# Retention and two feed-forward layers on one core: the first units in a new order, and two steps moved to ScalarE

## The chip, the cores and the metric

One NeuronCore of a Trainium2 chip runs the whole kernel. Its engines have in-order queues of their own and meet only at semaphores: TensorE (PE in the rows; PEld is its weight load), VectorE (DVE), ScalarE (ACT), GpSimd (POOL) and SyncE (SP), which here mostly issues DMAs. The metric is device time in microseconds (us). Times inside an execution come from one profiled execution and are counted from the start of its span.

## The reference

Three stages follow each other; all weights and activations are float32 with 4 batches, 8 heads, 768 positions, head size 64, so 3072 tokens of 512 features.

```
state = gamma[h] * state + k_t^T v_t ;  y_t = scale * q_t state      (retention, per head)
x = y laid out [3072, 512]
h = x @ w_in            [512 -> 2048]
g = h if h > 0 else exp(h) - 1
x = g @ w_out           [2048 -> 512]
h = x @ w_in2           [512 -> 1024]
s = h * softmax(h) ;  ln = (s - mean(s)) / sqrt(var(s) + 1e-6) * g_ln
out = ln @ w_out2       [1024 -> 512]
```

## The kernel before, in words

**Precision.** A large matmul is three matmuls on rounded halves: high times high, low times high, high times low (`mm3`, lines 68 to 72). So each operand is split: the high half is a cast on ScalarE (`xh`, `gh`, `w1ih`, `zh`), the low half a subtraction on VectorE (`xl`, `gl`, `w1il`, `zl`). The weights come as 64-bit words and pass through five steps for each tile of 128x512: `load_w` (a 512 KB DMA into one of five buffers `raw`), `top_w` (a cast on ScalarE into `top`, then a memset on GpSimd), `bits_w` and `merge_w` (VectorE shifts and ors), `high_w` (ScalarE), `low_w` (VectorE). `order1` is the list of the first layer's 32 tiles: `w1i` 0, 1, 2, then `w1o` 0, `w1i` 3, `w1o` 1 and so on. In the texts w0 to w7 are the tiles by place in that list, so w3 is the first tile of the output weights.

**Retention** works on 48 units, each 64 positions of one batch, loaded as one 576 KB DMA (`load_unit`, u0, u1, ...). Units 0 to 3 are the first chunks of the four batches, 4 to 7 the second chunks, and so on. For a unit TensorE makes scores (S, line 199), then the products of keys and values (K, 206) and the outputs (V, line 249, and from unit 4 on also 246, which reads the state that the unit four places earlier left). VectorE masks the scores (M, 210), makes the state (C, 221 or 223) and scales the output into `xf` (D, 254). ScalarE copies two halves of the state (226), GpSimd scales the keys (R, 190) and decays the state (G, 233). Every fp32 matmul of the program shows in the trace as two passes, so a group of 8 stands there as x16. The first eight units share three sets of PSUM banks in turn (`ab` and two named `acc`).

**First layer.** A block is 512 tokens, that is eight units; the block's matmuls need all eight units, split into `xh` and `xl` (`split_x0` for block 0). A step s makes the input matmul of one group of 128 hidden features (`ff1_in`, 12 matmuls into `hp`), ScalarE and VectorE make the nonlinearity (`elu_a`, `elu_b`, `elu_c`), and two steps later `ff1_out` adds 12 matmuls into `acc`. In the first block's steps the weights are prepared (`prep_w`), and every second step holds one unit of the next block.

**Second layer** goes by 24 tiles of 128 tokens. `norm_a` is exp, sum and product, then the subtraction of the mean on GpSimd (line 394). `turn` transposes in 32x32 blocks on VectorE (414) and writes to DRAM (`t_dr`), `turned` reads it back with four DMAs (`zt`); `split_zh` and `split_zl` make the halves, and `ff2_out` is 24 matmuls into `op`. `split_y` makes the halves of a later tile's input, which `load_y` reads.

**What sets the order.** The program is recorded in the order in which the Python code runs, and each engine keeps that order. The first units are written by a loop over u (lines 491 to 508) with three tables, LOADS, MID and END, which say after which unit a load, a weight step or a split of x stands:

```
LOADS = {0: (2, 3, "0"), 1: (4,), 2: (5,), 3: (6,), 4: (7, "1"), 5: (8,), 6: ("2", "3", 9), 7: ("4", 10)}
```

(numbers are units, strings weight tiles). Between, the loop writes for each u, in this order: R and G of unit u+1, C of u, S and M of u+1, V of u, K of u+1, D of u. All loads go out on SyncE's queue.

Of the kernel before, what the change touches and what calls it, by code (L numbers as in the profile page):

```python
# [40 lines left out]
HALF_N = 232  # L41


@with_exitstack
def tile_retention_ffn(ctx, tc, qkv, w_in1, w_out1, w_in2, w_out2, g_ln, dmask, odec, kgdec, ident_in, out):
# [16 lines left out]
    g_sb = small.tile([P, NF2], F32, name="g_sb")  # L62
    half_n = small.tile([P, HALF_N], F32, name="half_n")[:, :1]

# [9 lines left out]
    with tc.manual_schedule():  # L74
# [20 lines left out]

        def load_w(x):
            t = stage_p.tile([P, 512, 2], U32, tag="raw", name="raw")
            nc.sync.dma_start(out=t.rearrange("p a b -> p (a b)"), in_=srcs[x[0]][x[1]].bitcast(U32))
            raw_t[x] = t
# [11 lines left out]
        quarter = lambda x, i, dt: raw_t[x].rearrange("p a b -> p (a b)").bitcast(dt).rearrange("p (a b) -> p a b", b=4)[:, :, i]  # L111

        def top_w(x):
            top = tops[-1][0]
            tops[-1].reverse()
            nc.scalar.copy(top.bitcast(F16).rearrange("p (a b) -> p a b", b=2)[:, :, 1], quarter(x, 3, BF16))
            nc.gpsimd.memset(quarter(x, 3, U16), 0)  # L117
            top_t[x] = top

        def bits_w(x):  # L120
            raw = raw_t.pop(x)
            low, t = raw[:, :, 0], raw[:, :, 1]
            nc.vector.scalar_tensor_tensor(low, low, 29, top_t.pop(x), ALU.logical_shift_right, ALU.bitwise_or)
            abs_t[x] = low, t
# [56 lines left out]

        def load_unit(u):
            pool, n = (first_p, 4) if u < 4 or u == UPB - 1 else (at_p, 3)
            t = pool.tile([P, 18 * D], F32, tag="in", name="in", bufs=n)
            nc.sync.dma_start(out=t, in_=qkv[u])
            in_t[u] = t
# [25 lines left out]

        def att_state(u, v):

            c = chunk(u)
            if c == NCH - 1:
                return
            st = at_p.tile([P, 2, 2 * D], F32, tag="state", name="state", bufs=B + 1)
            kv = v[:, :, 4 * C:4 * C + 2 * D]
            if c == 0:  # L220
                nc.vector.tensor_copy(st, kv)
            else:
                nc.vector.tensor_tensor(st, sg_t.pop(u), kv, ALU.add)
            s2 = at_p.tile([P, 2 * D], F32, tag="s2", name="s2", bufs=B + 1)
            for j in range(2):
                nc.scalar.copy(s2[half(1 - j)], st[half(j), 1 - j])
            s_t[u + B] = (st, s2)

# [6 lines left out]
        def att_values(u, banks):  # L235
            c = chunk(u)
            t, pt = in_t.pop(u), p_t.pop(u)
            col = lambda o: slice(2 * C + o * C, 2 * C + (o + 1) * C)
            by_kind = heads(lambda x, y, z: (y if x == 0 else 1 - y, y, z))
            if c > 0:  # L240
                st, s2 = s_t.pop(u)
# [137 lines left out]
        def norm_a(i):  # L379
# [12 lines left out]
            nc.vector.tensor_scalar(st[:, 5:6], st[:, 4:5], -1.0 / FF2, None, ALU.mult)  # L392
            if i < N2 - 1:
                nc.gpsimd.tensor_scalar(z, z, st[:, 5:6], 1.0, ALU.add, ALU.mult)  # L394
# [55 lines left out]
        def ff2_out(i, kks=range(NF2)):  # L450
# [13 lines left out]

        w = lambda f, i: lambda: step_w(f, order1, i)
        xh = lambda *us: lambda: split_x0(us, True)
        xl = lambda *us: lambda: split_x0(us, False)

        LOADS = {0: (2, 3, "0"), 1: (4,), 2: (5,), 3: (6,), 4: (7, "1"), 5: (8,), 6: ("2", "3", 9), 7: ("4", 10)}
        MID = {4: (w(bits_w, 0),), 5: (w(merge_w, 0),), 6: (xl(0, 1, 2, 3),)}  # L470
        END = {
            3: (w(top_w, 0), xh(0, 1, 2, 3)),
            5: (w(high_w, 0), xh(4, 5)),
            6: (xh(6),),
            7: (xh(7), w(low_w, 0), w(top_w, 1), xl(4, 5), xl(6), xl(7), w(bits_w, 1), w(top_w, 2), w(merge_w, 1)),
        }
        nc.gpsimd.memset(half_n, -0.5)
        new_top()
        nc.sync.dma_start(out=kg_sb, in_=kgdec)
        load_unit(0)  # L480
        nc.sync.dma_start(out=dm_sb, in_=dmask)
        load_unit(1)
        nc.sync.dma_start(out=od_sb, in_=odec)
        new_acc(0)
        sets = [([x[:, 0], x[:, 1]], x) for x in (ab, *acc_t[0])]
        both = sets[0]
        scale_k(0)
        att_scores(0, sets[0][0])
        att_mask(0, sets[0][1])
        att_kv(0, sets[0][0])  # L490
        for u in range(UPB):
            banks, v = sets[u % 3]
            nxt, w = sets[(u + 1) % 3] if u + 1 < UPB else both
            for x in LOADS.get(u, ()):
                load_unit(x) if isinstance(x, int) else step_w(load_w, order1, int(x))
            scale_k(u + 1)
            if u + 1 >= B:
                att_decay(u + 1)
            att_state(u, v)
            att_scores(u + 1, nxt)  # L500
            att_mask(u + 1, w)
            att_values(u, banks)
            att_kv(u + 1, nxt)
            for f in MID.get(u, ()):
                f()
            att_done(u, v)
            for f in END.get(u, ()):
                f()
# [3 lines left out]
        att_state(UPB, both[1])  # L512
        scale_k(UPB + 1)
        att_decay(UPB + 1)
        step_w(high_w, order1, 1)
        step_w(bits_w, order1, 2)
        step_w(low_w, order1, 1)
        slot = 1
# [3 lines left out]
        for s in range(NS + LAG):  # L522
# [12 lines left out]
            if u < NU:  # L535
# [13 lines left out]
                if u + 2 < NU:  # L549
                    scale_k(u + 2)  # L550
            if tb == 0:
                prep_w(order1, slot)
                slot += 1
# [11 lines left out]
            if tb == 0:  # L565
                prep_w(order1, slot)
                slot += 1
                elu_c(s, nc.vector)
            if s == HL:
# [33 lines left out]
        for i in range(1, N2):  # L603
# [92 lines left out]
```

## Time and profile before

| what | value |
|---|---|
| median of 3 runs | 875.2 us (874.94 to 876.35) |
| the profiled execution's own time | 874.49 us |
| its span | 872.7 us |
| TensorE busy | 857.3 us, 98% of the span, 6432 matmul passes |
| VectorE, ScalarE, GpSimd busy | 438.7, 330.6, 322.8 us |
| DMA moved | 97.81 MB |

A share of 98% is a mean over stages. TensorE's missing 15 us lie almost all at the beginning, where it waits for loads and for the other engines, a little at one place of the second layer, and at the end. Idle time of another engine costs nothing while TensorE has work.

### The profile page before, as it was taken

What the parts mean: (1) busy time and instruction counts of PE and PEld (TensorE: products, weight loads), DVE (VectorE), ACT (ScalarE), POOL (GpSimd) and SP (SyncE); (2) the same over time, 40 slices, a digit from 0 to 9 for tenths busy, and PEclk for the clock granted to TensorE, in tenths of its full rate; (3) what the DMA queues carried; (4) which work ended last, traced back from release to release, by engine and by line L of the source; (5) the groups of instructions that cost most, each with busy time, mean ns of one, the idle gap of its engine ahead of it and who ended that gap; (6) DMA issues with size and microseconds to landing.
All of it is one profiled execution on the core that took longest, in us unless ns stands there. A gap on an engine that the chain in (4) does not pass through costs nothing.

```text
span 872.7 us, 15630 instructions
## 1 busy us (share of the span) xinstructions
PE 857.3 (98%) x6432; PEld 702.8 (81%) x6432; DVE 438.7 (50%) x736; ACT 330.6 (38%) x575; POOL 322.8 (37%) x321
## 2 busy tenths in 40 slices
PE   6899999999999999999999999999999999999998
PEld 5788888888888888888888878888788888888887
DVE  4899983222522233222422268796555555555552
ACT  3677762222322233222321245443343333333333
POOL 4555533322323232332322245553443333333330
PEclk9999999999999999999999999999999999999999
DMA  8677623111311113110311116310644444444432
GB/s 331 229 232 236 206 98 104 56 46 37 103 56 55 36 48 104 56 55 29 102 56 31 55 67 205 97 48 1 200 150 145 145 146 145 145 145 145 145 122 71
DMA packets 59735, 97.81 MB, mean 112 GB/s; under 512 B 4880, under 2 KB 41360, under 8 KB 59664
## 3 DMA queue, kind: packets, MB, share of 16 engines
q1 hardware_dynamic: 59664, 96.82, 34.0%
q8 instruction: 50, 0.82, 0.4%
q14 instruction: 21, 0.17, 0.1%
HBM read 72.16 MB, written 24.64 MB: 111 GB/s over the span
## 4 chain that ended last, share of the span: by engine, by line
PE 91%; DMA 3%; DVE 3%; ACT 1%; issue 1%; SPq 0%; POOL 0%; ACTq 0%; DVEq 0%
PE hp L71 14%; PE hp L72 14%; PE hp L70 14%; PE acc L70 11%; PE acc L72 10%; PE acc L71 10%; PE op L72 4%; PE op L70 4%; PE op L71 4%; PE ab L199 2%; DMA in<-in_qkv 2%; PE ab L206 1%; PE ab L246 1%; PE ab L249 1%; DMA zt<-t_dr 1%; DMA t_dr<-t 1%
## 5 line engine op out<-in xcount | busy, mean ns | idle before, releaser
L323 POOL TENSOR_TENSOR gl<-e,gh 128x512 fp32r<-128x512 f32 x80 | 106.9, 1336 | 310.9 <-issue 158.1
L70 PE MATMUL acc<-gh,w1oh 128*128 128x512 f32 x384 | 153.9, 401 | 0.4 <-ACT w1oh L138 0.4
L72 PE MATMUL acc<-gh,w1ol 128*128 128x512 f32 x384 | 150.0, 391 | 0.2 <-DVE w1ol L146 0.2
L71 PE MATMUL acc<-gl,w1oh 128*128 128x512 f32 x384 | 149.8, 390 | 0.0
L71 PE MATMUL hp<-xl,w1ih 128*128 128x512 f32 x380 | 147.9, 389 | 0.4 <-DVE xl L267 0.4
L70 PE MATMUL hp<-xh,w1ih 128*128 128x512 f32 x380 | 147.9, 389 | 0.0
L72 PE MATMUL hp<-xh,w1il 128*128 128x512 f32 x380 | 147.8, 389 | 0.0
L304 ACT ACTIVATE e<-hp 128x512 f32<-128x512 f32 x80 | 47.8, 597 | 186.0 <-PE hp L72 186.0
L313 DVE TENSOR_SCALAR e<-e 128x512 f32<-128x512 f32 x80 | 38.5, 481 | 136.3 <-ACT e L304 136.1
L315 ACT CAST gh<-e 128x512 fp32r<-128x512 f32 x96 | 59.6, 621 | 95.1 <-DVE e L314 82.7
L70 PEld LDWEIGHTS acc<-gh,w1oh 128*128 128x128 f32 x384 | 72.0, 188 | 17.1 <-ACT w1oh L138 0.8
L72 PEld LDWEIGHTS acc<-gh,w1ol 128*128 128x128 f32 x384 | 72.1, 188 | 15.9 <-DVE w1ol L146 0.6
L210 DVE TENSOR_TENSOR pt<-ab,dm_sb 128x256 f32<-128x256 f32 x43 | 18.1, 421 | 131.1 <-PE ab L249 124.6
L71 PEld LDWEIGHTS hp<-xl,w1ih 128*128 128x128 f32 x380 | 71.3, 188 | 15.7 <-DVE xl L267 0.9
L71 PEld LDWEIGHTS acc<-gl,w1oh 128*128 128x128 f32 x384 | 72.1, 188 | 14.0
L72 PEld LDWEIGHTS hp<-xh,w1il 128*128 128x128 f32 x380 | 71.3, 188 | 14.8
L70 PEld LDWEIGHTS hp<-xh,w1ih 128*128 128x128 f32 x380 | 71.3, 188 | 14.8
L117 POOL MEMSET raw<- 128x512 uint16 x48 | 61.0, 1279 | 48.7 <-DVE w1il L146 18.2
L394 POOL TENSOR_SCALAR z<-z,st 128x1024 f32<-128x1024 f32 x22 | 27.8, 1263 | 138.2 <-DVE st L392 138.2
L72 PE MATMUL op<-w2oh,zl 128*128 128x512 f32 (+1 forms) x192 | 74.2, 386 | 1.4 <-DVE zl L435 1.4
L70 PE MATMUL hp<-w2ih,yh 128*128 128x512 f32 x192 | 74.7, 389 | 0.0
L71 PE MATMUL hp<-w2il,yh 128*128 128x512 f32 x192 | 74.7, 389 | 0.0
(118 smaller groups left out, 1411.7 us busy)
## 6 DMA issues: line engine op xcount, KB each, us to landing
in<-in_qkv SPq DMA_DIRECT2D x48, 576.0 KB, 4.2
raw<-in_w_in SPq DMA_DIRECT2D x24, 512.0 KB, 3.8
raw<-in_w_out SPq DMA_DIRECT2D x24, 512.0 KB, 4.1
t_dr<-t SPq DMA_DIRECT2D x22, 512.0 KB, 2.8
zt<-t_dr SPq DMA_DIRECT2D x88, 128.0 KB, 2.5
y_dr<-yt SPq DMA_DIRECT2D x24, 256.0 KB, 2.7
yin<-y_dr SPq DMA_DIRECT2D x24, 256.0 KB, 3.4
out<-ot SPq DMA_DIRECT2D x23, 256.0 KB, 2.8
```

Source lines behind the costliest of these rows:

```text
L70: nc.tensor.matmul(o, lh, rh, start=first, stop=False)
L71: nc.tensor.matmul(o, lh, rl, start=False, stop=False)
L72: nc.tensor.matmul(o, ll, rh, start=False, stop=last)
L117: nc.gpsimd.memset(quarter(x, 3, U16), 0)
L199: nc.tensor.matmul(banks[j][half(a), m * C:(m + 1) * C], blk(t, j, K, n), blk(t, j, Q, n), start=True, stop=True)
L206: nc.tensor.matmul(banks[a][half(j), 4 * C + m * D:4 * C + (m + 1) * D], blk(t, a, KR, n), blk(t, a, V, n), start=True, stop=True)
L210: nc.vector.tensor_tensor(pt, v[:, :, :2 * C], dm_sb, ALU.mult)
L304: nc.scalar.activation(e, h_t[s], AF.Exp)
L313: nc.vector.tensor_scalar(e, e, 1.0, -1.0, ALU.min, ALU.add)
L315: nc.scalar.copy(gh, e)
L323: engine.tensor_tensor(gl, e, gh.bitcast(F32), ALU.subtract)
L394: nc.gpsimd.tensor_scalar(z, z, st[:, 5:6], 1.0, ALU.add, ALU.mult)
```

## The change

The loop and its tables are replaced by one string of operations, START, which a table STEP maps to the functions; the letters are those used above, with L a unit's load, w a weight load, t, b, m, h, o the steps top, bits, merge, high and low, H and X the high and low split of x. `l` and `v` are a unit's and a weight's load issued from ScalarE's queue. A second string, LATER, stands in step 0 of the first layer. Parts that are new beside the order: the states of units 0 to 3 are copied out of PSUM by ScalarE and not by VectorE; the copies of state halves of units 4 to 8 are split off (`att_copy`) and put later; the loads of w4 and of unit 10 are issued by ScalarE; for every fourth tile of `order1` (places 1, 5, 9, ...) ScalarE makes the last bits with an activation in place, and the VectorE step `bits_w` falls away; and in the second layer tile 1's mean is subtracted by ScalarE, after `split_zl(0)`, with its transpose ahead of `split_y(3)`.

```
+START = """
+    n a z L0 k d L1 q L2 L3
+    R0 S0 M0
+    R1 S1 M1 V0 K0 C0 D0 L4 L5 w0
+    R2 S2 M2 V1 K1 C1 D1 L6 L7 H0 w1
+    R3 G4 S3 M3 V2 K2 C2 D2 H1
+    R4 S4 G5 M4 V3 K3 C3 D3 H2 t0
+    V4 D4 R5
+    S5 M5 K4 L8 C4 V5 R6 b0 S6 M6 m0 h0 K5 D5 G6 R7 H3 H4
+    S7 V6 M7 D6 V7 R8 t1 w2 H5 H6 D7 H7 C5 K6 C6 S8 K8 K7 X0,1 X2,3
+    o0 b1 m1 h1 X4,5 X6,7 t2 w3 L9 G8 G7 o1 b2 t3 M8 b3 C8 R9 c4 v4
+"""
+LATER = "m2 h2 C7 l10 G9"
...
         def top_w(x):
+            if x in order1[1::4]:
+                nc.scalar.activation(quarter(x, 0, U16), quarter(x, 1, U16), AF.Identity, bias=floor_n, scale=2.0 ** -13)
+                nc.scalar.copy(quarter(x, 1, F16), quarter(x, 3, BF16))
+                nc.gpsimd.memset(quarter(x, 3, U16), 0)
+                return
...
-            nc.vector.scalar_tensor_tensor(low, low, 29, top_t.pop(x), ALU.logical_shift_right, ALU.bitwise_or)
+            if x in top_t:
+                nc.vector.scalar_tensor_tensor(low, low, 29, top_t.pop(x), ALU.logical_shift_right, ALU.bitwise_or)
...
             if c == 0:
-                nc.vector.tensor_copy(st, kv)
+                nc.scalar.copy(st, kv)
...
+        def late_w(i):
+            done.add((load_w, order1[i]))
+            load_w(order1[i], nc.scalar)
...
+        for x in START.split():
+            STEP[x[0]](*(int(n) for n in x[1:].split(",") if n))
...
+            if s == 0:
+
+                for x in LATER.split():
+                    STEP[x[0]](*(int(n) for n in x[1:].split(",") if n))
+            if 0 < s < B + 1:
+                att_copy(B + s)
...
+                if s == 0:
+                    step_w(merge_w, order1, slot)
+                    step_w(high_w, order1, slot)
...
-            if i < N2 - 1:
+            if i == 1:
+                pass
+            elif i < N2 - 1:
                 nc.gpsimd.tensor_scalar(z, z, st[:, 5:6], 1.0, ALU.add, ALU.mult)
...
                 split_zl(0)
+                z, _, st = zc_t[1]
+                nc.scalar.activation(z, z, AF.Identity, bias=st[:, 5:6])
+                turn(1)
+                turned(1)
             if i + 2 < N2:
                 split_y(i + 2)
-            if i < N2 - 1:
+            if 1 < i < N2 - 1:
                 turn(i)
                 turned(i)
```

**TensorE just ahead of the first layer.** Before, the last groups of the first stretch (line 206 makes K, 199 S, 246 and 249 V) are, for units 5 to 8:

```order
L206 MATMUL ab<-in 64x64 x8
L199 MATMUL acc<-in 64x64 x8
L246 MATMUL ab<-in,state 64x64 x4
L246 MATMUL ab<-in,s_225 64x64 x4
L249 MATMUL ab<-pt,in 64x64 x8
L206 MATMUL acc<-in 64x64 x8
L199 MATMUL ab<-in 64x64 x8
L246 MATMUL acc<-in,state 64x64 x4
L246 MATMUL acc<-in,s_262 64x64 x4
L249 MATMUL acc<-pt,in 64x64 x8
L206 MATMUL ab<-in 64x64 x8
```

Now (222 is S, 229 K, 274 and 277 V):

```order
L222 MATMUL acc<-in 64x64 x8
L274 MATMUL ab<-in,state 64x64 x4
L274 MATMUL ab<-in,s_257 64x64 x4
L277 MATMUL ab<-pt,in 64x64 x8
L274 MATMUL acc<-in,state 64x64 x4
L274 MATMUL acc<-in,s_293 64x64 x4
L277 MATMUL acc<-pt,in 64x64 x8
L229 MATMUL ab<-in 64x64 x8
L222 MATMUL ab<-in 64x64 x8
L229 MATMUL ab<-in 64x64 x8
L229 MATMUL acc<-in 64x64 x8
```

The same groups stand there in all, but V of units 6 and 7 follow each other, and three K groups (units 6, 8 and 7) come last, ahead of the first `hp` matmul.

**ScalarE in the first steps.** In step 1 of the first layer, before (301 and 302 are the exponential of step 1's `hp`, 226 the state copies, 138 `high_w`, 116 `top_w`, 315 `gh`):

```order
L315 CAST gh<-e 128x512
L138 CAST w1ih<-raw 128x512
L116 CAST top<-raw 128x512
L301 ACTIVATE e<-hp 128x512
L302 ACTIVATE e<-e 128x512
L226 COPY s_612<-state 64x128 x2
L138 CAST w1oh<-raw 128x512
```

Now (161 is `high_w`, 138 `top_w`, 343 `gh`, 329 and 330 the exponential, 113 and 208 loads):

```order
L255 COPY s_340<-state 64x128 x2
L113 DMA raw<-in_w_in 128x1024
L329 ACTIVATE e<-hp 128x512
L330 ACTIVATE e<-e 128x512
L161 CAST w1ih<-raw 128x512
L208 DMA in<-in_qkv 128x1152
L343 CAST gh<-e 128x512
L138 CAST top<-raw 128x512
L161 CAST w1oh<-raw 128x512
L329 ACTIVATE e<-hp 128x512
```

The high half of w3 (`w1oh`) has moved ahead of the second exponential and its state copies, and two loads, of w4 and of unit 10, stand in this queue now; the cast just ahead of `w1oh` is `top_w` of w4.

**VectorE at tile 1 of the second layer.** Before (391 is the product z of tile 1, 435 `zl` of tile 0, 366 `yh` of tile 3, 414 the transpose of tile 1):

```order
L391 SCALAR_TENSOR_TENSOR z,st<-hp_6095,st,e_6121 128x1024
L392 TENSOR_SCALAR st<-st 128x1
L435 TENSOR_TENSOR zl<-spare,zh 128x4x8x32
L366 CAST yh<-yin 128x512
L414 STREAM_TRANSPOSE t<-z 128x1024
```

Now:

```order
L419 SCALAR_TENSOR_TENSOR z,st<-hp_6102,st,e_6128 128x1024
L420 TENSOR_SCALAR st<-st 128x1
L465 TENSOR_TENSOR zl<-spare,zh 128x4x8x32
L444 STREAM_TRANSPOSE t<-z 128x1024
L394 CAST yh<-yin 128x512
```

The transpose has gone ahead of `yh`. Its input is finished by ScalarE now, between `zh` of tile 0 and the square of tile 1, and no longer by GpSimd.

## Rows read from the trace of the kernel before

**Rows 1.** Windows: us, busy us of each engine (xinstructions), granted clock, DMA share, GB/s.
```profile
0.00:40.00 40.00, 29.92 (x583) 24.28 (x584) 24.90 (x49) 19.40 (x40) 20.80 (x31) 1.00 0.79 290
40.00:150.00 110.00, 110.00 (x1068) 89.59 (x1068) 92.24 (x157) 74.83 (x131) 53.31 (x51) 1.00 0.56 179
```

**Rows 2.** Timeline of PE, 0 to 31 us: start, us, engine, line, operation; idle before it.
```profile
9.15 0.71 PE L199 MATMUL acc<-in 64*64 64x64 f32 x16
...
14.58 0.73 PE L206 MATMUL acc<-in 64*64 64x64 f32 x16 [0.21 <-POOL sg L233]
...
20.43 0.37 PE L206 MATMUL ab<-in 64*64 64x64 f32 x2 [0.43 <-issue]
...
26.84 0.48 PE L206 MATMUL ab<-in 64*64 64x64 f32 x6 [1.51 <-issue]
27.25 0.79 PE L292 MATMUL hp<-xh,w1ih 128*128 128x512 f32 x1
...
30.40 0.39 PE L292 MATMUL hp<-xh,w1il 128*128 128x512 f32 x1
```

**Rows 3.** DMA queues in windows 12.6:12.7, 18.0:18.1, 24.3:24.4: packets, MB, share.
```profile
q8 instruction: 1, 0.02, 60.1%
...
q8 instruction: 1, 0.02, 59.2%
...
q8 instruction: 1, 0.02, 55.4%
```

**Rows 4.** DMA issues in windows 4.2:4.3, 4.7:4.75, 31.0:31.1: KB, us to landing.
```profile
raw<-in_w_in SPq DMA_DIRECT2D x1, 512.0 KB, 7.6
...
in<-in_qkv SPq DMA_DIRECT2D x1, 576.0 KB, 8.5
...
raw<-in_w_in SPq DMA_DIRECT2D x1, 512.0 KB, 3.5
```

**Rows 5.** Timeline of PE where the first output matmuls begin, 38 to 40 us.
```profile
38.09 0.39 PE L72 MATMUL hp<-xh,w1il 128*128 128x512 f32 x1
38.83 0.50 PE L70 MATMUL acc<-gh,w1oh 128*128 128x512 f32 x1 [0.36 <-ACT w1oh L138]
...
39.75 0.50 PE L72 MATMUL acc<-gh,w1ol 128*128 128x512 f32 x1 [0.19 <-DVE w1ol L146]
```

**Rows 6.** Timelines of ACT and DVE at the same place.
```profile
38.12 0.66 ACT L138 CAST w1oh<-raw 128x512 fp32r<-128x512 f32 x1
38.68 0.79 ACT L116 CAST top<-raw 128x512 f16<-128x512 bf16 x1
...
39.02 0.68 DVE L146 TENSOR_TENSOR w1ol<-raw,w1oh 128x512 fp32r<-128x512 f32 x1
```

**Rows 7.** Timeline of PE in the second layer, tile 1's output, 631 to 634 us.
```profile
631.23 0.39 PE L71 MATMUL hp<-w2il,yh 128*128 128x512 f32 x1
631.46 0.39 PE L72 MATMUL hp<-w2ih,yl 128*128 128x512 f32 x1
632.13 0.50 PE L70 MATMUL op<-w2oh,zh 128*128 128x512 f32 x1 [0.28 <-ACT zh L429]
...
633.39 0.50 PE L72 MATMUL op<-w2oh,zl 128*128 128x512 f32 x1 [0.53 <-DVE zl L435]
```

**Rows 8.** The chain that ended last, 622.6 to 631 us: start, us, what.
```profile
622.66 1.16 DVE t L414
623.84 2.77 DMA t_dr<-t
...
627.99 2.94 DMA zt<-t_dr
```

**Rows 9.** Timelines of POOL, DVE and ACT at tile 1, 619 to 623 us.
```profile
619.96 2.10 POOL L394 TENSOR_SCALAR z<-z,st 128x1024 f32<-128x1024 f32 x1 [6.30 <-DVE st L392]
...
619.84 1.23 DVE L435 TENSOR_TENSOR zl<-spare,zh 128x1024 fp32r<-128x1024 f32 x1
...
622.10 1.06 ACT L403 ACTIVATE e<-z 128x1024 f32<-128x1024 f32 x1 [2.48 <-POOL z L394]
```

More of the change, by code (lines that the diff above doesn't have):

```diff
@@ L62, in tile_retention_ffn @@
     g_sb = small.tile([P, NF2], F32, name="g_sb")
-    half_n = small.tile([P, HALF_N], F32, name="half_n")[:, :1]
+    half_n = small.tile([P, HALF_N], F32, name="half_n")
+    floor_n, half_n = half_n[:, 1:2], half_n[:, :1]
     t_dr = [dram.tile([4, 4, 32, 2 * P], F32, name=f"t_dr{i}") for i in range(3)]
@@ L94, in tile_retention_ffn, with load_w @@
         dsts = {"w1i": w1i, "w1o": w1o, "w2i": w2i, "w2o": w2o}
-        def load_w(x):
+        def load_w(x, queue=nc.sync):
             t = stage_p.tile([P, 512, 2], U32, tag="raw", name="raw")
-            nc.sync.dma_start(out=t.rearrange("p a b -> p (a b)"), in_=srcs[x[0]][x[1]].bitcast(U32))
+            queue.dma_start(out=t.rearrange("p a b -> p (a b)"), in_=srcs[x[0]][x[1]].bitcast(U32))
             raw_t[x] = t
@@ L180, in tile_retention_ffn, with load_unit @@
         blk = lambda t, p, base, n: t[half(p), base + n * D:base + (n + 1) * D]
-        def load_unit(u):
+        def load_unit(u, queue=nc.sync):
             pool, n = (first_p, 4) if u < 4 or u == UPB - 1 else (at_p, 3)
             t = pool.tile([P, 18 * D], F32, tag="in", name="in", bufs=n)
-            nc.sync.dma_start(out=t, in_=qkv[u])
+            queue.dma_start(out=t, in_=qkv[u])
             in_t[u] = t
@@ L211, in att_mask, with att_state @@
             p_t[u] = pt
-        def att_state(u, v):
+        def att_state(u, v, copy=True):
             c = chunk(u)
@@ L224, in att_state, with att_copy @@
             s2 = at_p.tile([P, 2 * D], F32, tag="s2", name="s2", bufs=B + 1)
+            s_t[u + B] = (st, s2)
+            if copy:
+                att_copy(u)
+        def att_copy(u):
+            st, s2 = s_t[u + B]
             for j in range(2):
                 nc.scalar.copy(s2[half(1 - j)], st[half(j), 1 - j])
-            s_t[u + B] = (st, s2)
         def att_decay(u):
@@ L236, in att_values @@
             c = chunk(u)
-            t, pt = in_t.pop(u), p_t.pop(u)
+            t, pt = in_t[u], p_t.pop(u)
             col = lambda o: slice(2 * C + o * C, 2 * C + (o + 1) * C)
@@ L240, in att_values @@
             if c > 0:
-                st, s2 = s_t.pop(u)
+                st, s2 = s_t[u]
                 for j, a, m in by_kind:
@@ L462, in ff2_out @@
                 del zt_t[i], op_t[i]
[L465 to L483, printed above, removed]
+        def late_w(i):
+            done.add((load_w, order1[i]))
+            load_w(order1[i], nc.scalar)
         new_acc(0)
@@ L486, in tile_retention_ffn @@
         both = sets[0]
[L487 to L508, printed above, removed]
+        of = lambda u: sets[u % 3] if u < UPB else both
+        STEP = {
+            "L": load_unit, "l": lambda u: load_unit(u, nc.scalar),
+            "S": lambda u: att_scores(u, of(u)[0]), "K": lambda u: att_kv(u, of(u)[0]),
+            "V": lambda u: att_values(u, of(u)[0]), "M": lambda u: att_mask(u, of(u)[1]),
+            "D": lambda u: att_done(u, of(u)[1]), "C": lambda u: att_state(u, of(u)[1], u < B), "c": att_copy,
+            "R": scale_k, "G": att_decay, "H": lambda *u: split_x0(u, True), "X": lambda *u: split_x0(u, False),
+            "w": lambda i: step_w(load_w, order1, i), "v": late_w, "t": lambda i: step_w(top_w, order1, i),
+            "b": lambda i: step_w(bits_w, order1, i), "m": lambda i: step_w(merge_w, order1, i),
+            "h": lambda i: step_w(high_w, order1, i), "o": lambda i: step_w(low_w, order1, i),
+            "k": lambda: nc.sync.dma_start(out=kg_sb, in_=kgdec), "d": lambda: nc.sync.dma_start(out=dm_sb, in_=dmask),
+            "q": lambda: nc.sync.dma_start(out=od_sb, in_=odec),
+            "z": new_top, "n": lambda: [nc.gpsimd.memset(a, b) for a, b in ((half_n, -0.5), (floor_n, 2.0 ** -14 - 0.5))],
+            "a": lambda: nc.scalar.copy(sm_p.tile([P, 1], F32, tag="rs", name="rs"), half_n),
+        }
+        for x in START.split():
+            STEP[x[0]](*(int(n) for n in x[1:].split(",") if n))
         first.close()
@@ L511, in tile_retention_ffn @@
         g_p = ph1.enter_context(tc.tile_pool(name="g", bufs=3, reuse_waits="tile"))
[L512 to L517, printed above, removed]
         slot = 1
```

## The prediction

> **What bounds the kernel now.** I read the busy time by stretches first, then TensorE's own timeline where it is not busy all the time, then for each stop there the engine that released it. From 40 to 150 us TensorE is busy 110.00 of 110 us, though VectorE with 92.24 us is not far from full; in the first 40 us it is busy 29.92 [rows 1]. So the kernel's time is the matmuls, plus what is lost before the first layer runs, plus single stops. Three places can be moved by this change.
>
> The first is the start. The first layer's first matmul stands at 27.25 us, and two stops before it are put down to "issue", 0.43 us before 20.43 and 1.51 us before 26.84, both in the middle of a K group [rows 2]. No semaphore ends them. In the DMA queues a queue "instruction" moves one packet of 0.02 MB at 12.6, 18.0 and 24.3 [rows 3], the last two about 2.4 and 2.5 us before the stops end. From one stop to the next TensorE does the last 4 passes of a K group, S of unit 7 (16), V of 6 (32), K of 7 (16), S of 8 (16), V of 7 (32) and 10 of K of 8: 126 passes. Each is a weight load and a matmul, so 252 instructions, with the few waits among them about 256. I take it that TensorE's program comes in pages of that size, and that the next page but one is asked for when a page is entered. Counted back by 126 passes from 20.43, a page is entered 14 passes into the K group of 14.58, at 14.58 + 14 x 0.028 = 14.97 (two passes last 0.37 us and six 0.48, so one more adds 0.028 and a group of 16 holds TensorE for 0.45); by another 126, at the end of the S group of 9.15, at 9.55 [rows 2]. The packets follow these entries by 3.05, 3.0 and 3.9 us [rows 3]. So a page, while the DMA engines are full of loads, takes at most 5.42 us (9.55 to 14.97, with no stop seen), then 5.46 (14.97 to 20.43), then 6.41 (20.43 to 26.84).
>
> The Trainium skill, Runtime: NRT & Kernel Launch, section Instruction fetch mechanics, says that instructions are refilled in 16 KiB blocks of 256 while the current one runs, and that the cost of a crossing is mostly hidden. The trace agrees on the size; it does not agree on hidden, with 0.43 and 1.51 us lost. By that rule the start would go as in the first rival below.
>
> The second place is the first output matmuls: from 38.09 to 39.75 are 1.66 us for three matmuls, which at the 0.23 us between matmuls back to back (631.23 to 631.46, [rows 7]) take 0.68, so 0.98 us are lost, first to w3's high half on ScalarE, then to its low half on VectorE [rows 5, 6]. The third is tile 1 of the second layer: 631.46 to 633.39, 1.93 us for three matmuls, 1.25 lost to `zh` and `zl` of that tile [rows 7].
>
> **The change part by part.**
>
> The start. The order now has S0, S1, V0, K0, S2, V1 as its first 96 passes, so the first page ends with V1 and not with S of unit 2: one group later, 0.45 us. Against that unit 0's load is issued first, ahead of the small one, some 0.4 us earlier; if half of that reaches unit 2, the entry comes at about 9.55 + 0.45 - 0.2 = 9.8 us (9.5 to 10.0). The 222nd pass is now 14 passes into V of unit 4, the 348th 12 passes into S of unit 7, the 474th 10 passes into the K group of unit 7, which is the last before the first layer, just as K of unit 8 is now. For the three pages I take 5.42, 5.46, and for the third the mean of 5.46 and 6.41, 5.9, since the loads of w4 and unit 10, which stood in the queue then, are issued later now. 9.8 + 5.42 + 5.46 + 5.9 = 26.6, and six passes more, 0.17: the first layer begins at 26.7, against 27.25. Gain 0.55 us; with 5.4 for each page and 9.5 it is 25.9 (gain 1.4), with 6.41 and 10.0 it is 27.5 (loss 0.2).
>
> What the order moves otherwise hides behind these pages. Units 4 and 5 are loaded ahead of w0; w0 is landed before (4.2 + 7.6 = 11.8) one transfer ahead of unit 4 (4.7 + 8.5 = 13.2) [rows 4], so units 4 and 5 come about 1.3 us earlier, and w0 some 2.7 later, at 14.5. The four state copies on ScalarE take the place of VectorE's; 128x256 from PSUM is not shown on ScalarE, and between nothing and the 0.66 us of a 128x512 cast [rows 6] I take 0.45. D of the unit waits behind each of them now, and S three units later behind D; these waits lie before 15 us, ahead of the page that ends there. w1's bits on ScalarE are an activation beside the cast: between -0.2 and +0.8 us each against one cast of 0.79 [rows 6]; I take 0.8, before the high half of w1, which is due only after twelve matmuls of the first layer. The first eight of these matmuls start 0.45 us apart on a mean (27.25 to 30.40 for seven steps, [rows 2]), twice the later 0.23: the lower of the clock's two levels, 1.2 GHz, until TensorE had worked on them for 3.15 us. I leave that as it is; if the rise came at the same clock time, 30.40, an earlier start would give back half of itself, 0.3 us, and without the slow stretch 1.5 more would be won.
>
> The first output matmuls. w3's high half leaves the place behind the second exponential and the state copies: it is made in step 0's end, behind w4's `top`. VectorE has w3's merge ahead of step 1's work, and one `bits` step less, 0.7 us if it takes no more than the low half does. Before, the high half starts at 38.12 [rows 6]; now it needs step 0's exponential, w2's high half, `gh` and w4's cast, step 0's matmuls end at 26.7 + 3.15 + 5 x 0.23 = 31.0, and with two activations and then four casts, 0.66 to 0.79 us each [rows 6], it is there at about 35.3; the low half waits for VectorE's bits of w4 too and comes under two us after, at 37. TensorE wants them at 38.32 - 0.55 = 37.8 and 38.2. All 0.98 us go; with the low half late by a little, 0.7. What is next late is the tile after (w4), on the same engines; VectorE reaches it sooner by the step that left it.
>
> Every fourth tile. In each 12 us of the first block VectorE loses one step of 0.7 us or more, ScalarE has one of 0.8 more. TensorE has no stop from 40 to 150 us [rows 1], so this is worth nothing there; and ScalarE, 74.83 of 110 us busy, has room for seven times 0.8.
>
> Tile 1. Before: GpSimd's subtraction, 619.96 and 2.10 us long, then on VectorE `yh` of tile 3, then the transpose at 622.66, its write at 623.84 with 2.77 us, the reads, of which the last lands at 627.99 + 2.94 = 630.93 [rows 8, 9]. Now ScalarE subtracts: it is free then, and an activation of 128x1024 takes 1.06 us there, so 619.9 to 621.0; VectorE has `zl` of tile 0 until 621.1 [rows 9]; the transpose starts at 621.1 in place of 622.66, 1.55 us earlier, and the write and the reads with it: landed at 629.4, `zh` at 630.5, and `zl` of tile 1 behind the transpose of tile 2, which also comes about 1.1 us earlier, done at 631.9. TensorE wants them at 631.69 and 632.15. The whole 1.25 us go. Bounds: nothing, if the reads land no earlier, and 1.25, since the matmuls behind are dense.
>
> The sum is 0.55 + 0.98 + 1.25 = 2.8 us. The profiled execution took 874.49 us (span 872.7), so 871.7; the median of the runs is 875.2, 0.7 above it, which gives 872.4.
>
> **The rivals.**
>
> The pages are hidden (the rule above): they come in time, because fewer loads stand before them. Then the two stops of 0.43 and 1.51 us go whole, 1.94 us, and the earlier units, 1.3 us, reach the end of the chain in part: the first layer begins between 24.1 and 25.3, 2.0 to 3.1 us earlier. With the other two gains, 0.98 and 1.25, that is 4.2 to 5.3 us: 869.9 to 871.0, middle 870.4. For it: two of the moved loads leave the queue. Against: units 8 and 9, w2 and w3 are still issued there, and 12.6 and 18.0 show the same delay at different loads.
>
> Only tile 1 is won, or only it and half of the rest: w3's halves are still late (VectorE works without a pause before them), and the start stays. 875.2 - 1.25 = 873.9, up to 874.9 if the transpose's write meets other transfers.
>
> ScalarE's queue turns into the bound. Place: `top` of w4, ahead of w3's high half. w4's load is issued by ScalarE itself behind w3's cast and the last state copies, ahead of step 0's exponential, so at 31.0 at the latest (the end of step 0's matmuls). With the 3.5 us of a load on a quiet queue it is there at 34.5; with the 8.5 us of a full one [rows 4], at 39.5. Behind it wait the high half (0.66, after the cast's 0.79) and on VectorE the bits of w4 and the low half of w3 (0.7 each): the low half would be there at 39.5 + 0.8 + 0.7 + 0.7 = 41.7 in place of 39.75. That is 1.95 us lost, whatever the start has won, and 1.25 won at tile 1: 875.9. It decides from a landing at 38.8 on. Against it: the DMA queue drains by 27 us or so.
>
> **How the numbers follow.** The forecast has a chance of 0.50, with a range of its own of 871.2 to 873.4; hidden pages 0.24; only part won 0.19; ScalarE's queue 0.07. A measurement of this kernel tells 0.2%, 1.75 us, from no change, so faster means below 873.45: 0.47 of the forecast, 0.24 and 0.04 of the third case make 0.75; same is 0.19; slower 0.06. The range goes from 869.3 (hidden pages with a clock that rises early) to 874.7.
>
> **What would show it.** Right: an "issue" stop in the last K group before the first `hp` matmul, that matmul at 26.7, instruction packets some 3 to 4 us after the 96th, 222nd and 348th pass, no stop at the first `acc` matmuls of the first layer, none at tile 1's `op`, and w4 landed before 35 us. Wrong: an `hp` matmul at 25 or earlier without such stops; a stop that names `w1oh`, `top` or `zl` of tile 1; a new stop between 40 and 150 us.

## The result, and the profile after

The changed kernel takes 881.45 us (median of 4 runs, 880.1 to 882.91) against 875.25 us (4 runs, 874.94 to 876.35): ratio 1.0072, 95% interval [1.0054, 1.0091]. It is slower by 6.2 us where 2.8 faster was forecast, and outside the range. The profiled execution took 882.91 us, span 881.1, 8.4 us more than that of before.

The busy time by stretches, as in [rows 1] (us, then busy us of PE, PEld, DVE, ACT and POOL, granted clock, DMA share, GB/s):

```profile
0.00:40.00 40.00, 27.15 (x580) 23.10 (x581) 21.33 (x43) 20.80 (x44) 18.86 (x31) 0.79 0.77 275
40.00:150.00 110.00, 107.69 (x980) 82.64 (x979) 86.63 (x146) 87.63 (x141) 51.15 (x48) 1.00 0.53 179
```

From 40 to 150 us TensorE did 1068 operations before and 980 now, and ScalarE's 74.83 us have become 87.63. That is the first sign: the loss lies in the stretch that I had called full. The next table gives the start of the same matmul in the profile of before, and how much later it comes in the changed kernel, in e10 (the changed kernel again) and in e1 (all bits by VectorE), both below. It shows how the loss grows:

```
same matmul                    before   changed  changed again  all bits by VectorE
first hp                        27.25    +0.49      +1.01           +1.38
first hp of step 1              31.56    +1.47      +0.86           +2.08
third group of first outputs    40.79    +0.73      -0.24           +0.97
first hp of step 9              78.76    +4.77      +3.87           +1.34
first hp of step 17            128.88    +7.62      +6.68           +1.34
first op of tile 1             632.13    +8.20      +6.41           +0.89
third op of tile 1             633.39    +8.20      +5.61           +0.11
span                           872.7    881.1      878.2           872.9
```

So 6.9 us are lost between 40.79 and 128.88: 5.6 of them a little in every second step, mostly in gaps too short for the timeline to name, and 1.3 in the first step of the next block, most of it at one stop. The place where it begins is TensorE's timeline after the first outputs (start, us, engine, line, operation; idle before it), which also answers to [rows 5]; the last row is that stop:

```profile
40.16 0.39 PE L85 MATMUL acc<-gh,w1oh 128*128 128x512 f32 x1
40.38 0.39 PE L86 MATMUL acc<-gl,w1oh 128*128 128x512 f32 x1
...
42.65 0.39 PE L87 MATMUL acc<-gh,w1ol 128*128 128x512 f32 x1
43.72 0.50 PE L85 MATMUL hp<-xh,w1ih 128*128 128x512 f32 x1 [0.68 <-ACT w1ih L161]
...
131.00 0.50 PE L86 MATMUL hp<-xl,w1ih 128*128 128x512 f32 x1 [0.86 <-DVE xl L295]
```

The stops at `acc` are gone, as forecast. But the next `hp` stands and waits for `w1ih`. ScalarE's timeline at the same time says why (its last row belongs to the stop at 131.00):

```profile
39.82 1.48 ACT L132 ACTIVATE raw<-raw,half_n 128x512 uint16<-128x512 uint16 x1
41.33 1.37 ACT L133 CAST raw<-raw 128x512 f16<-128x512 bf16 x1
42.42 0.71 ACT L343 CAST gh<-e 128x512 fp32r<-128x512 f32 x1
43.01 0.66 ACT L161 CAST w1ih<-raw 128x512 fp32r<-128x512 f32 x1
...
48.13 0.63 ACT L343 CAST gh<-e 128x512 fp32r<-128x512 f32 x1 [0.67 <-DVE e L339]
...
128.29 2.18 ACT L290 CAST xh<-xf 128x512 fp32r<-128x512 f32 x4
```

L132 and L133 are the two steps that make a fourth tile's last bits: 2.85 us, where one cast of 0.79 stood [rows 6]. ScalarE works in order, and `gh` and `w1ih` are behind them. In a step without them ScalarE still waits 0.67 us for VectorE's `e` ahead of `gh` (the row of 48.13); in a step with them it waits for nothing, and `w1ih` is late. How much room the steps with them had is seen in the kernel before, where the same `gh` comes behind a single cast:

```profile
40.33 0.63 ACT L315 CAST gh<-e 128x512 fp32r<-128x512 f32 x1 [0.86 <-DVE e L311]
```

It is 0.86 to 0.87 us in each of these steps (the other steps have 0.66 to 0.68). The two steps need 2.06 us more than the cast. The stop at 131.00 is the same delay carried on: `xl` needs `xh` of the next block, which ScalarE begins at 128.29, and at 119.60 before.

The start, answering to [rows 2]:

```profile
8.13 0.70 PE L222 MATMUL acc<-in 64*64 64x64 f32 x16 [2.95 <-DMA in<-in_qkv]
...
9.88 0.71 PE L222 MATMUL acc<-in 64*64 64x64 f32 x16 [0.19 <-DMA in<-in_qkv]
10.36 0.65 PE L277 MATMUL acc<-pt,in 64*64 64x64 f32 x16
...
15.94 0.21 PE L274 MATMUL acc<-in,s 64*64 64x64 f32 x1 [1.28 <-issue]
...
20.78 0.37 PE L222 MATMUL acc<-in 64*64 64x64 f32 x2 [0.90 <-issue]
...
27.33 0.48 PE L229 MATMUL acc<-in 64*64 64x64 f32 x5 [1.66 <-issue]
27.74 0.79 PE L320 MATMUL hp<-xh,w1ih 128*128 128x512 f32 x1
```

The "issue" stops stand at the predicted passes (14 into V of unit 4, 12 into S of unit 7, 11 into K of unit 7, one more than said). But V1, the end of the first page's passes, ends later than I had put it (10.36 + 0.43 = 10.8, not 9.8), since S of unit 1, at 7.21 before, waits 2.95 us for its load and comes at 8.13. The three pages then take 16.5 us, close to the 16.8 of the forecast, and the first `hp` comes 1.0 us later than forecast.

Tile 1's output, answering to [rows 7], with SyncE's DMA issues ahead of it:

```profile
640.33 0.50 PE L85 MATMUL op<-w2oh,zh 128*128 128x512 f32 x1 [0.70 <-ACT zh L459]
...
641.59 0.50 PE L87 MATMUL op<-w2oh,zl 128*128 128x512 f32 x1 [0.53 <-DVE zl L465]
```

```profile
630.07 0.37 SPq L446 DMA_DIRECT2D t_dr<-t  x1
634.69 1.74 SPq L452 DMA_DIRECT2D zt<-t_dr  x4
```

Both stops are still there. The write `t_dr` is issued earlier against the matmuls around it, but it is 4.62 us from its issue to the first read, where before it was 2.84 (the write took 2.77 of them [rows 8]).

### The profile page after: what moved, and what is told of

Read it like the earlier page. It is cut to its first block, busy times and chain, and to the rows that moved or that the text cites. A ratio compares the mean times of both kernels' runs of the same rounds, so it can differ in the third digit from the quotient of the medians.

```text
span 881.1 us, 15619 instructions
## 1 busy us (share of the span) xinstructions
PE 860.3 (98%) x6432; PEld 701.0 (80%) x6432; DVE 431.5 (49%) x724; ACT 348.3 (40%) x593; POOL 319.3 (36%) x321
## 4 chain that ended last, share of the span: by engine, by line
PE 82%; ACT 6%; DVE 6%; DMA 2%; issue 2%; SPq 1%; POOL 0%; DVEq 0%; ACTq 0%
PE hp L86 13%; PE hp L87 13%; PE hp L85 13%; PE acc L85 9%; PE acc L87 8%; PE acc L86 8%; PE op L87 4%; PE op L86 4%; PE op L85 4%; PE ab L222 2%; ACT raw L132 1%; ACT raw L133 1%; DVE gl L351 1%; PE ab L274 1%; ACT w1oh L161 1%
## 5 line engine op out<-in xcount | busy, mean ns | idle before, releaser
L86 PEld LDWEIGHTS hp<-xl,w1ih 128*128 128x128 f32 x380 | 71.5, 188 | 16.8 <-DVE xl L295 2.2
L85 PE MATMUL op<-w2oh,zh 128*128 128x512 f32 (+1 forms) x192 | 74.2, 386 | 0.9 <-ACT zh L459 0.9
L87 PE MATMUL hp<-w2ih,yl 128*128 128x512 f32 x192 | 74.7, 389 | 0.0
```

What stands on the lines that cost most here:

```text
L85: nc.tensor.matmul(o, lh, rh, start=first, stop=False)
L86: nc.tensor.matmul(o, lh, rl, start=False, stop=False)
L87: nc.tensor.matmul(o, ll, rh, start=False, stop=last)
```

## The experiments

Each run stands beside runs of the kernel before on the same chip: e1 to e4 (median 874.72 of 29 runs), e5 to e8 (875.11 of 29), e9 to e12 (876.37 of 8). What is compared across these groups is the ratio.

**e1: all last bits by VectorE, the rest of the change kept.**

```
 def top_w(x):
-    if x in order1[1::4]:
-        (ScalarE's two steps, the memset) ; return
```

> The changed kernel with VectorE making the last bits of all 32 tiles again, all else as changed. Theory A (ScalarE's two steps per fourth tile, 1.46 and 1.37 us in place of 0.77, hold TensorE up from 43 us on): no stops named w1ih between 43 and 130 us, about 5.5 us less than the changed kernel, so 875.5 to 876.5. Rival B (the new order itself leaves the first block short, and the bits only show it): the stops from 43 us on stay, above 879.

872.68 us (12 runs), ratio 0.9979 [0.9968, 0.9991]: under even theory A's range, and rival B falls. The bits cost 8.8 us by the medians, 8.1 by the ratios, and without them the change is faster than before. From 40 to 150 us the timeline of TensorE names no stop. The profile of the changed kernel places 6.9 us of the cost; the rest can't be placed, since e1's profiled execution took 874.69, 2.0 above its median, with a late start. ScalarE at the place of the rows above:

```profile
40.18 0.78 ACT L133 CAST top<-raw 128x512 f16<-128x512 bf16 x1
41.13 0.62 ACT L338 CAST gh<-e 128x512 fp32r<-128x512 f32 x1 [0.17 <-DVE e L334]
41.74 0.68 ACT L156 CAST w1ih<-raw 128x512 fp32r<-128x512 f32 x1
```

There is idle time ahead of `gh`, so VectorE's `e` sets the pace and not the queue. It is only 0.17 here, and 0.67 in the next such step, because the new order has put four state copies (1.23 us) ahead where the later steps have two (0.61); in the later ones it is 0.86 to 0.88, as before.

**e2: the kernel before with the bits on ScalarE and nothing else** (the same `if` block put into `top_w`).

> The kernel before with only ScalarE's bits for every fourth tile. Theory A: TensorE gets stops behind ScalarE at every second step of the first block, 4 to 6 us in all, 879.5 to 881.5. Rival B: ScalarE has room (74.83 of 110 us busy before), within 0.5 us of 875.2.

880.6 us (6 runs), ratio 1.0062 [1.0043, 1.008], as theory A had it. The loss comes with this one part, whatever the start; in the profile it grows from nothing at 40.79 us to 5.1 at 128.88.

**e3: the kernel before with tile 1 centred on ScalarE and nothing else.**

```
-if i < N2 - 1:          # norm_a: centre on POOL
+if i == 1: pass
+elif i < N2 - 1:
...
+    z, _, st = zc_t[1]
+    nc.scalar.activation(z, z, AF.Identity, bias=st[:, 5:6])
+    turn(1); turned(1)
```

> The kernel before with only tile 1 of the second layer subtracted on ScalarE and transposed earlier. Theory C (the earlier write meets TensorE's instruction packet of 16 KB on one of the DMA engines and waits for it): the write of tile 1 takes 4 us or more in place of 2.8, the stops at tile 1's output stay over 0.8 us, 874.8 to 875.3. Rival D (in the changed kernel the write was slow by chance): the write takes 2.8 us, no stops there, 873.9 to 874.1.

873.83 us (12 runs), ratio 0.9988 [0.9974, 1.0003]: by the runs alone not told from no change. In its profile both stops at tile 1 are gone and the matmuls behind gain 1.14 us; the write's issue to the first read takes 2.92. So theory C falls for this kernel.

**e4: 50 matmuls of zeros ahead of the kernel before's first scores,** to move the places where TensorE's instruction pages end.

```
+zero = tops[-1][0].bitcast(F32)
+for _ in range(50):
+    nc.tensor.matmul(ab[:D, 0, :C], zero[:D, :D], zero[:D, D:D + C], start=True, stop=True)
```

> The kernel before with 50 fp32 matmuls of 64x64 on zeros ahead of the first scores, while TensorE waits for the first load: 100 passes, so that each boundary of 256 instructions stands 100 passes earlier in the real work, and the first page is entered before the loads fill the DMA engines. Theory E (the two issue stops are waits for program pages, asked for on entry of the page before): no stop of 1.5 us ahead of the first hp matmul, which begins between 25.3 and 26.2, 873.3 to 874.3. Rival F (the stops come from the load on the DMA engines at those times whatever the place in the program): stops at 20 and 25 to 27 us stay, the first hp matmul at 27.2, 875.2.

878.39 us (12 runs), ratio 1.0042 [1.0026, 1.0057]; the first `hp` comes at 29.61. Neither theory gave this time: the extra passes did not fit into TensorE's idle time.

```profile
1.32 10.82 PE L489 MATMUL ab<-top 64*64 64x64 f32 x99 [1.32 <-POOL top L108]
11.84 0.38 PE L199 MATMUL ab<-in 64*64 64x64 f32 x3
...
21.94 0.28 PE L246 MATMUL acc<-in,s 64*64 64x64 f32 x4 [0.36 <-issue]
...
29.61 0.50 PE L292 MATMUL hp<-xh,w1ih 128*128 128x512 f32 x1 [0.44 <-ACT xh L277]
```

They took 10.82 us, so the units began at 11.84 and not at 5.22. Two things can be read all the same. The stop at 21.94 stands behind 349 passes, the 100 of zeros counted, and the one at 20.43 in the kernel before behind 348 [rows 2]: it kept its count and met other work, which speaks for theory E's fixed places and against rival F. And from the first score to the first `hp` are 17.8 us here and 22.0 before, with one "issue" stop of 0.36 in place of 0.43 and 1.51 [rows 2]. With loads and instructions there, and with the clock at its upper level, 2.4 GHz, from 18.9 us on (a group of 16 passes takes 0.41 to 0.46 us there, 0.65 to 0.71 in the kernel before), the units took 4 us less; how much of that is each one's is not shown. Why a pass of zeros took 0.108 us stays open.

**e5: the two steps write into a `top` tile,** one 16-bit number every 4 bytes, and not in place into `raw`, one every 8.

```
-nc.scalar.activation(quarter(x, 0, U16), quarter(x, 1, U16), ...)
-nc.scalar.copy(quarter(x, 1, F16), quarter(x, 3, BF16))
+half_of = lambda dt: top.bitcast(dt).rearrange("p (a b) -> p a b", b=2)
+nc.scalar.activation(half_of(U16)[:, :, 0], quarter(x, 1, U16), ...)
+nc.scalar.copy(half_of(F16)[:, :, 1], quarter(x, 3, BF16))
```

> The changed kernel, with ScalarE's two steps of every fourth tile written into a top tile (a 16-bit number every 4 bytes) in place of the raw tile itself (one every 8 bytes, in place). Theory A (what cost the time is how long ScalarE's in-order queue is held ahead of the cast w1ih, and the spacing or the in-place write makes the two steps 1.46 and 1.37 us): both steps take 0.75 to 0.85 us, some 1.6 us in all against 0.78 for the one cast, so 0.8 us more where ScalarE has 0.67 us of idle time a step; nearly all stops of hp on w1ih go, 873 to 875.5 us. Rival B (the steps' kind and their input's spacing make them slow): ACTIVATE stays near 1.46 us, the cast is 0.78, in all 2.25; stops of about half the size, 876 to 879 us.

873.85 us (12 runs), ratio 0.9985 [0.9975, 0.9996]. The two lines of it (ns min/median/max, first and last start, form):

```profile
L134 ACT ACTIVATE top<-raw,half_n x8: 872/886/892, 20.7 to 110.9; 128x512 uint16<-128x512 uint16 x8
...
L135 ACT CAST top<-raw x8: 747/752/767, 21.4 to 111.7; 128x512 f16<-128x512 bf16 x8
```

1.64 us in place of 2.85, and 7.6 us of the 8.8 are back. ScalarE now has 0.85 us more to do at each fourth tile than with the cast alone, just within the 0.86 that it has idle in most of these steps. The profile shows 1.0 us lost from 40.79 to 128.88, e1's 0.4. Both lose it ahead of the first `hp` of step 7 (66.97 here), behind the two steps that have less room (0.17 and 0.67 in e1); from there to 128.88 neither loses anything.

**e6: no such steps, but longer casts.** e1 with the cast of every fourth tile made three and a half times.

```
+for n in (512, 512, 512, 256) if x in order1[1::4] else (512,):
     nc.scalar.copy(top...[:, :n, 1], quarter(x, 3, BF16)[:, :n])
```

> e1 (all tiles' last bits by VectorE) with the cast of every fourth tile made three and a half times over, into the same top tile: the same data at the end, 2.7 us of ScalarE in place of 0.78, about what the two steps of the changed kernel took (2.83). Theory A (time in ScalarE's queue, nothing else): the stops of hp on w1ih come back at every second step, 877.5 to 882 us. Rival C (the loss comes from the two steps' own writes into raw, by contention or by what waits for them, not from the time in the queue): as e1, 872 to 874 us.

880.85 us (6 runs), ratio 1.0069 [1.0052, 1.0086]: the changed kernel's time to 0.6 us, with VectorE doing all the bits. The profile loses 7.8 us from 40.79 to 128.88, in the same steps. Rival C falls: it is the time in ScalarE's queue.

**e7: w3's halves early, alone.**

```
     slot += 1
+    if s == 0:
+        step_w(merge_w, order1, slot)
+        step_w(high_w, order1, slot)
     elu_c(s, nc.vector)
```

> The kernel before with one part of the change: the fourth tile's merge and high half made ahead of elu_c in the first step. Theory: the stops of the first output matmuls (0.98 us of the prediction's sum; 1.09 measured in the changed kernel's trace) go and stay gone, 873.4 to 874.2 us against 874.7 of the kernel before. Rival: the gain is given back at a wait behind it, 874.5 to 875.2 us.

875.02 us (12 runs), ratio 0.9995 [0.9984, 1.0007]: no gain to be measured, as the rival had it, but for another reason. The profile shows half of the stops left:

```profile
40.74 0.50 PE L72 MATMUL acc<-gh,w1ol 128*128 128x512 f32 x1 [0.35 <-DVE w1ol L146]
```

The high half is in time, the low half is not: VectorE makes it at 40.01, behind another tile's bits. In the changed kernel the new list had moved those bits too, and all went, so the 1.09 us are not this edit's alone.

**e8: w3's halves early and tile 1 on ScalarE, old start** (e7's and e3's edits together).

> The kernel before with the fourth tile's merge and high half early and tile 1 centred on ScalarE, with the old start and all last bits by VectorE. If the two gains stand apart and add (0.98 + 1.14 us by the traces): 872.3 to 873 us, as fast as e1 with its new start (872.68), which then has no part in e1's gain. If the new start has a part in e1's 2.0 us: 873.3 to 874.5 us.

873.73 us (12 runs), ratio 0.9979 [0.9968, 0.999], the ratio of e1. In microseconds that is in the second range, but the kernel before was 0.4 us slower beside it too. The ratios are equal, so the runs show no part of the new start in e1's gain; with intervals of 1 us to either side they don't exclude one.

**e9: the spacing alone.** e1 with six half-width instructions more at each fourth tile.

```
+pick = lambda dt, b: top.bitcast(dt).rearrange("p (a b) -> p a b", b=b)[:, :256, 1]
+cast(pick(F16, 2)); cast(pick(F16, 4)); act(pick(U16, 2)); act(pick(U16, 4))
...
+cast(quarter(x, 3, F16)[:, :256]); act(quarter(x, 3, U16)[:, :256])
```

> A measurement of durations alone: e1 with six half-width ScalarE instructions (128x256) more at every fourth tile, whose results are overwritten: the cast and the integer ACTIVATE, each writing 16-bit numbers every 4 bytes into top, every 8 bytes into top, and every 8 bytes in place into raw. If the spacing of what is written makes the steps slow, both 8-byte forms take 0.65 to 0.8 us and the 4-byte ones 0.4 to 0.45; if it is writing into the tile that is read, only the in-place forms take long and the 8-byte form into top takes 0.4 to 0.45.

One run (899.07 us), read for its durations. In each first row of the two lines the two spacings are mixed, one of each; the smallest is the 4-byte form, the largest the 8-byte form:

```profile
L134 ACT CAST top<-raw x16: 471/638/790, 21.3 to 132.9; 128x256 f16<-128x256 bf16 x16
L134 ACT CAST raw<-raw x8: 758/768/772, 24.9 to 136.1; 128x256 f16<-128x256 bf16 x8
...
L135 ACT ACTIVATE top<-raw,half_n x16: 582/734/877, 22.6 to 134.3; 128x256 uint16<-128x256 uint16 x16
L135 ACT ACTIVATE raw<-raw,half_n x8: 860/862/876, 25.7 to 136.9; 128x256 uint16<-128x256 uint16 x8
```

Every 8 bytes costs the same into `top` (0.79 and 0.88 at most) as in place (0.77 and 0.86); every 4 bytes 0.47 and 0.58. The 4-byte forms and the ACTIVATE are somewhat longer than expected. What is read lies 8 bytes apart in all six. So it is the spacing of what is written, and not the writing in place.

**e10: the changed kernel once more.**

> The changed kernel once more, for a second profile. Theory D (tile 1's gain was lost because an instruction packet for TensorE lay among the packets of tile 1's write, where it falls from one execution to the next): the packet falls elsewhere, the write's issue to the first read of zt is 2.8 to 3.0 us in place of 4.6, and the two stops ahead of tile 1's output are gone. Rival (the new place of the step brings packet and write together each time): 4 us or more again. The first hp matmul comes anywhere from 26.9 to 28.7 us.

880.01 us, one run. The write and its reads, and tile 1's first matmul:

```profile
629.10 0.37 SPq L446 DMA_DIRECT2D t_dr<-t  x1
632.53 1.74 SPq L452 DMA_DIRECT2D zt<-t_dr  x4
```

```profile
638.31 0.39 PE L87 MATMUL hp<-w2ih,yl 128*128 128x512 f32 x1
638.54 0.39 PE L85 MATMUL op<-w2oh,zh 128*128 128x512 f32 x1
```

The instruction packet fell elsewhere, 2.86 us after the write's issue, when the write's packets end. 3.43 us are more than the 3.0 expected, and still there is no stop: tile 1's gain is in the changed kernel too (1.2 us from 6.85 ahead of it to 5.61), and its first profile had lost it.

**e11: e1 with K8 behind the first layer's first twelve matmuls.**

```
-    ... C6 S8 K8 K7 X0,1 X2,3
-    o0 b1 m1 h1 ... M8 b3 C8 R9 c4 v4
+    ... C6 S8 K7 X0,1 X2,3
+    o0 b1 m1 h1 ... M8 b3 R9 c4 v4
-LATER = "m2 h2 C7 l10 G9"
+LATER = "K8 m2 h2 C7 C8 l10 G9"
```

> e1 with the 16 kv passes of unit 8 (K8) and their state (C8) moved from ahead of the first hp matmuls to behind the first twelve of them. Theory P (in both starts the first hp matmul waits for the third set of TensorE's instructions to land, at 26.8 to 28.2 us, and nothing else): 11 of the 12 hp matmuls now stand ahead of that stop, the first hp comes at 24.5 to 25.5 us, the stop lies behind it, and the time is 1 to 3 us under e1's, 869.7 to 871.7. Rival Q (what bounds the start lies behind, in VectorE's and ScalarE's making of w1il and of the second tile's halves): hp starts early and waits for these, 872 to 873.5.

871.28 us (5 runs), ratio 0.9944 [0.9929, 0.9958], the fastest kernel here, 5.1 us under the kernel before on its chip.

```profile
20.22 0.27 PE L217 MATMUL acc<-in 64*64 64x64 f32 x2 [0.96 <-issue]
...
24.22 0.79 PE L315 MATMUL hp<-xh,w1ih 128*128 128x512 f32 x1
24.96 0.80 PE L315 MATMUL hp<-xh,w1il 128*128 128x512 f32 x1
...
28.12 1.14 PE L315 MATMUL hp<-xl,w1ih 128*128 128x512 f32 x4
29.42 0.46 PE L224 MATMUL ab<-in 64*64 64x64 f32 x16 [0.16 <-DVE pt L228]
29.81 0.50 PE L85 MATMUL hp<-xh,w1ih 128*128 128x512 f32 x1
```

With the sixteen passes behind them, eleven of the twelve `hp` matmuls stand ahead of the page's end. The first comes at 24.22, earlier even than the 24.5 to 25.5 of theory P, and the time is in its range. The "issue" stops behind the 222nd and 348th pass are still there (1.17 and 0.96 us); the last one, right ahead of the first `hp` in e1, is gone. Of the 3.0 us that the first `hp` is earlier than before, 1.75 are kept at the first `hp` of step 1, since the sixteen passes now stand between, 2.2 at 129 us and 3.4 behind tile 1.

**e12: e11, and the first tile's low half ahead of the first xl** (`o0` put before `X0,1`).

> e11 and, beside it, the first tile's low half (o0, 0.68 us of VectorE) made ahead of the first xl (1.57 us) and not behind. Theory P: w1il no longer holds the second hp matmul (VectorE ends it at 25.48 in e1, here near 24.0), so some 0.5 to 1 us under e11 if e11 shows a stop there, 869 to 871. Rival Q: as e11, since xl comes later by 0.7 us: 872 to 873.5.

872.23 us (5 runs), ratio 0.9952 [0.9939, 0.9965]. The gap at the second `hp` matmul goes (24.89 behind 24.29, 0.60 us where e11 has 0.74), and nothing is won by it: 872.23 against 871.28 us, not told apart by five runs each. Theory P's addition falls here, and the time is rival Q's.

## Why the prediction was wrong

**The step that failed** is "Every fourth tile". It said that ScalarE had a step of 0.8 us more, that TensorE had no stop from 40 to 150 us and that ScalarE, 74.83 of 110 us busy, had room for seven times that, so that it was worth nothing there. It cost 8.8 us by the medians (881.45 against e1's 872.68). What it had wrong is first of all the price: the two steps take 2.85 us and not 1.6, 2.06 more than the cast and not 0.8, because they write a 16-bit number every 8 bytes (e5, e9). The price had been taken from a cast with the same input and half the spacing in its output. The argument on the room was wrong too: a share of busy time over 110 us says nothing of one place in an in-order queue. The room is the idle time right ahead of `gh`, 0.86 us in each of these steps (the row of 40.33 before), and [rows 1] does not hold it. With 2.06 us more, ScalarE, and not VectorE's `e`, sets when `gh` and `w1ih` come. e6 shows this with casts in place of the bits: as long a time in ScalarE's queue loses as much. That the 0.8 would have fitted is luck: it is 0.06 under a room that I had not looked up, and e5, with 0.85, loses 0.6 us more than e1 behind the two steps in which the new order had made that room smaller, and nothing more from step 7 on. The new stop between 40 and 150 us was among the prediction's own signs of being wrong.

**The start.** 0.55 us were forecast for it. In five profiles of the old start (before, e2, e3, e7, e8) the first `hp` comes at 26.50 to 27.89, in five of the new one (both of the changed kernel, e1, e5, e6) at 26.95 to 28.63. The term is smaller than the difference from one execution to the next, and its sign was not borne out. The reading behind it was right: the last "issue" stop, 1.38 to 3.76 us in these ten, ends six passes or fewer ahead of the first `hp` each time, and in e11, which puts these matmuls ahead of the page's end, the first `hp` comes 3 us earlier. (The working counts with the next page being asked for on entry, a packet 3.05 us behind the entry at 9.55 and the page entered 5.42 behind it; the words "the next page but one" do not fit it.) By the Trainium skill, Runtime: NRT & Kernel Launch, section Instruction fetch mechanics, the cost of such crossings is mostly hidden; no profile here agrees for the start, since each has at least one "issue" stop of 0.36 us or more there, and e11 and e12 hide the last crossing alone. In the changed kernel's profile the slow clock lasted longer too. Its granted clock:

```profile
16.80:33.70 16.90, 13.38 (x238) 11.47 (x239) 12.32 (x25) 7.80 (x14) 11.14 (x13) 0.50 0.72 258
33.80:40.00 6.20, 6.20 (x87) 4.95 (x86) 5.06 (x9) 5.66 (x13) 2.28 (x3) 1.00 0.56 180
```

It is at 1.2 GHz up to 33.7, 6.0 us into the `hp` matmuls, which start 0.43 us apart there. Before, they stood 0.43 apart for 3.15 us [rows 2]. [rows 1] prints a granted clock of 1.00 for that stretch, but the trace of before holds no record of the clock ahead of 30.39 us, where its first one, of the upper level, begins; so the prediction read the lower level from the spacing alone. The longer slow stretch is the 1.0 us between the first `hp` and that of step 1. In the second profile it did not cost anything (+1.01, then +0.86), so it is no property of the order.

**The first output matmuls.** 0.98 us were forecast, and 1.1 came (from +1.84 to +0.73, again +0.87 to -0.24). The term was right. That it belongs to the early halves alone was not: the profile of e7 has 0.5 of it.

**Tile 1.** 1.25 us were forecast; 1.14 came in e3, 1.2 in the changed kernel's second profile and in e8. In its first profile they were lost to a write of 4.62 us. An instruction packet lay in the write's time, and behind it one of the 16 DMA engines alone still moved the write's packets. The DMA queues at 630.8 to 632.5 us, and the stretch behind:

```profile
q1 hardware_dynamic: 496, 0.49, 82.0%
q8 instruction: 1, 0.02, 6.2%
```

```profile
632.80:634.20 1.40, 1.40 (x8) 1.17 (x7) 1.05 (x3) 0.25 (x2) 0.22 (x1) 1.00 0.07 21
```

6.2% is one of sixteen, and the share of 0.07 is about one too. That the packet is the cause is read from its place, not shown: no run moved it by itself, and the other profiles speak for it only in part. In all of them an instruction packet starts within 3 us of this write's issue. Where it starts from 0.06 us ahead of the issue to 2.2 behind it, the six writes took 3.20 to 4.62 us to the first read; where it starts earlier or later, the other eight took 2.84 to 3.43. But the next tile's write, which no such packet comes near, took 2.79 to 2.93 in eleven profiles and 3.28 to 3.58 in three.

**The rivals.** That ScalarE's queue becomes the bound had 0.07, and it is what happened, at another place than the one that I named: not once at w4's load (w4 landed at 30.8, 4.3 us after its issue), but at every second step. The time, 881.45, is far from the 875.9 that this rival gave. That pages are hidden, with 0.24, fell.

## What to carry to other kernels

Before work is moved to an engine with a low busy share, look in its timeline for the idle time right ahead of the instruction that another engine waits for; that, and not the share, is the room. Price a moved step by a row with the same spacing in its output as well as the same shape. Where a stop for instructions stands at a fixed count of instructions, as here behind the 348th pass and the 474th or 475th, move work that is not urgent behind it (e11), rather than reorder what is ahead of it.

## What was not expected of the hardware

- ScalarE with 16-bit output: 128x512 every 4 bytes 0.75 us (cast) and 0.89 (integer ACTIVATE), every 8 bytes 1.37 and 1.47; at 128x256 0.47 and 0.58 against 0.77 and 0.86, in place or not.
- The stop for TensorE's instructions ahead of the first layer is 1.4 to 3.8 us long in kernels with the same start (1.66 and 2.92 in two executions of the changed one), so one profile can't price a reordering of half a microsecond there.
- The write of a tile `t_dr` (512 KB) took 2.8 to 4.6 us from its issue to the first read of it in 14 profiles; the cause of the longer ones is open.
- The granted clock stayed at 1.2 GHz for the first 6.0 us of `hp` matmuls in the changed kernel and for 2.8 in a second execution of it, which lost nothing there.
